# Reordering queries inside the score matmuls of an attention and channel-mix kernel

## The chip, the cores and the metric

One core of a Trainium2 chip runs the whole program. The metric is device time in microseconds (us) of one execution; a smaller number is better. The profiled execution is one run of the same program under the hardware profiler.

## What is computed

The reference is a block-causal attention followed by an RWKV channel mix, in these shapes: 8 batches, 8 heads, 576 tokens, 64 values a head; 512 channels, 1024 hidden channels.

```python
scores = (q @ k.T) / sqrt(64)                 # q, k, v: [8, 8, 576, 64]
scores = where(block_i >= block_j, scores, -1e9)   # blocks of 64 tokens
attn   = exp(scores - max) ; attn = attn / (attn.sum(-1) + 1e-9)
x      = (attn @ v).transpose(0, 2, 1, 3).reshape(8, 576, 512)
x_prev = x shifted by one token within its batch (zeros first)
xk = mu_k * x + (1 - mu_k) * x_prev
xr = mu_r * x + (1 - mu_r) * x_prev
k  = relu(xk @ w_k)                           # w_k: [512, 1024]
out = sigmoid(xr @ w_r) * ((k * k) @ w_v)     # float32 [8, 576, 512]
```

## The kernel before

**Stages.** For every batch, q and k are loaded, cast to bf16 and turned so that the 64 head values lie on the partitions. The first two batches (`TURNED = 2`) are turned by TensorE and evacuated (L462, tiles `q...` in the order list); the other six by a DMA transpose out of `NB` tiles. The result `t_qkt` holds, for every pair of heads, the queries and the keys. v is cast to fp16 into `VO`.

`add_score` makes the scores of one pair of heads in three PSUM tiles of 2 x 512 columns (`s{b}{pr}{0..2}`, L644 for the first 512 queries, L652 for the last 64), one head on the upper 64 rows of TensorE and one on the lower. The keys are the stationary operand, the queries the moving one. `J = 4` and `M = 128`: the 512 queries of a batch are cut by position p (0 to 127) and phase j (0 to 3), token = 4p + j. A piece of keys `kc` needs positions from 32 kc on, so the pieces have 512, 384, 256 and 128 columns. ScalarE takes exponentials of each tile into `t_e` in fp16 (L671), and GpSimd zeroes a masked corner (L680).

`add_values` then forms, per batch and half of the heads, the sums of the exponentials (`den`, names `d`/`e`; stationary `FOURTH` and `ONES`, four 32-column tiles of the array side by side) and three value products (`v{b}{Q}{i}`, stationary `VO`), all at L717. The sums put phase j on output partition group j, so VectorE takes reciprocals of 128 columns (L769), spreads the four phases into `t_rd` by `stream_shuffle` (L778), and `norm` (L824, L826, L813) multiplies the values by them into `t_xt`, which is float32 and in token order.

The channel mix works on chunks of 512 tokens: `d` is x minus its shift (L898, VectorE or GpSimd), `xk` and `xr` are formed on VectorE (L911), GpSimd fixes the batch borders (L926), TensorE multiplies by `WK` (L949, names `k`) and `WR` (L984, `r`), ScalarE applies relu (L960) and tanh (L995), the square (L969 or L967) goes to any of three engines, TensorE multiplies by `WV` (L1015, `p`), and VectorE joins the halves (L1027).

**Order before the change of the queries' layout.** In `t_qkt` the two turned batches hold queries in token order, and the other six hold them by phase: all positions of phase 0, then phase 1, and so on. Before, the scores and exponentials of every batch stand by phase. The turned batches therefore step through their queries four elements apart, and the others read them in a row:

```python
ask[:, 0:CUT].rearrange(
    "d (p j) -> d j p" if b < TURNED else
    "d (j p) -> d j p", j=J)[:, :, a:z],
```

The sums read each phase in a row, `probs(...)[:, j]`, and `norm` reads PSUM and `t_rd` by position and phase, 128 float32 apart, to write tokens in a row.

**What sets the order of the work.** `TENSOR` is a hand-written list of TensorE's tasks. `WHERE` says which engine does each task that could run on several (`flex`). `Plan` replays this list with a price for each task, ring buffers and semaphore latencies, and from that fixes the order of the instructions on each engine. The prices are written in the kernel (for example 0.215, 0.235 and 0.255 for the three score tiles, 0.75 for a sum of later batches). `FILL` matmuls keep TensorE occupied at the start until the first `k` task.

Of the kernel before, what the change touches and what calls it, by code (L numbers as in the profile page):

```python
# [24 lines left out]
q000 q010 q001 q011 s000 q030 q020 s0t0 s001 s010 q031 s012 s011 q021 s030 d00  # L25
s020 v000 s002 q100 q110 s022 d01 s021 q101 e00 s031 s0t1 q121 q111 v010 v001
q130 s032 q131 q120 v002 s1t0 k00 k03 e01 s100 s102 k01 v012 v011 s130 k02
s110 k04 s101 k15 s112 k06 k13 k07 s120 s111 k10 k14 k17 r01 k16 r00 k11 k05
s132 s121 k12 d10 v100 r11 s1t1 r10 s131 s122 v102 v101 p01 p10 d11 s200 v111
v110 v112 s201 s202 p00 p11 s210 s212 k20 k26 k21 s2t0 s220 r22 s211 r20 r21  # L30
r23 s230 k22 s232 k24 k23 k25 s222 k27 s221 d20 s231 p23 s2t1 v200 v201 v202
d21 s300 s302 p21 v210 v211 p20 v212 s310 s312 p22 s320 s3t0 k30 k34 k31 s330
s301 k32 k33 k35 s311 s331 r30 r33 s3t1 k37 k36 s321 s332 d30 r32 s322 r31 p31
d31 p33 p32 v300 v302 v301 v311 v312 s400 s402 v310 p30 s4t0 s420 s401 s410
k40 k43 k42 s412 s411 k41 r43 k45 k47 r42 s4t1 s422 k44 s421 k46 r40 d40 v402
v400 s430 s432 p42 s431 v401 r41 s500 d41 s501 p43 p40 v410 v411 v412 s530
s531 p41 s520 s532 r53 r52 s522 s521 k50 k56 s510 s5t1 k53 k52 k54 k57 s5t0
s512 k55 r51 k51 r50 s502 s511 d51 p50 d50 p53 s6t0 v502 v500 v510 v501 v511
s610 s611 p51 v512 s612 s6t1 p52 s600 s601 k60 k67 k64 k61 s620 s602 r60 k66
r63 k63 r61 d60 s630 s632 k65 r62 k62 s631 s621 v600 v601 v602 s622 p60 p63  # L40
s700 d61 v612 v610 v611 s701 s702 p62 s710 s711 p61 s730 s731 r70 k70 r72 s712
k72 k75 s7t0 s720 k76 r73 s7t1 s722 d70 v700 v701 s732 s721 r71 k77 k74 k73
k71 v702 d71 v710 v711 p71 p72 p73 p70 v712 k80 k84 k87 k83 k85 r81 k81 k86
k82 r83 r80 r82 p83 p82 p81 p80 r91 k90 k92 k91 k96 k94 r92 k93 k97 k95 r93
r90 p92 p90 p91 p93b p93a
# [4 lines left out]
    "ACT": "ev000 ev001 ev010 ev011 ev020 ev101 ev111 qk0000 qk0011 qk1101 "  # L50
            "qk1111 qk211 qk220 qk231 qk311 qk320 qk331 qk400 qk500 qk521 qk531 "
            "qk601 qk611 qk720 qk730 qk731 sq05 sq15 sq16 sq20 sq21 sq35 sq36 "
            "sq40 sq43 sq46 sq52 sq55 sq67 sq71 sq72 sq74 sq75 sq76 sq81 sq87 "
            "sq92 sq94 sq95 v00 v02 v03 v10 v11 v12 v30 v32 v51 v53 v60 v72 v73 "
            "wk0 wk1 wk4 wv0 wv4 wv5",
    "DVE": "d00 d01 d02 d03 d13 d20 d23 d32 d43 d50 d52 d71 d72 d81 d82 d83 "
            "d90 d91 d93 ev021 ev030 ev031 ev100 ev110 ev120 ev121 ev130 ev131 "
            "qk0010 qk0110 qk201 qk221 qk301 qk310 qk330 qk421 qk511 qk520 "
            "qk530 qk610 qk620 qk621 qk630 qk700 qk701 sq00 sq01 sq02 sq03 sq04 "
            "sq06 sq12 sq13 sq24 sq26 sq37 sq41 sq42 sq44 sq47 sq51 sq53 sq54 "  # L60
            "sq57 sq61 sq63 sq65 sq70 sq82 sq83 sq90 sq91 v01 v04 v13 v23 v31 "
            "v33 v42 v43 v44 v50 v52 v54 v61 v62 v63 wk2 wk3 wk5 wk6 wr3 wv2 "
            "wv3 wv6",
    "POOL": "d10 d11 d12 d21 d22 d30 d31 d33 d40 d41 d42 d51 d53 d60 d61 d62 "
            "d63 d70 d73 d80 d92 qk0001 qk0100 qk0101 qk0111 qk1000 qk1001 "
            "qk1010 qk1011 qk1100 qk1110 qk200 qk210 qk230 qk300 qk321 qk401 "
            "qk410 qk411 qk420 qk430 qk431 qk501 qk510 qk600 qk631 qk710 qk711 "
            "qk721 sq07 sq10 sq11 sq14 sq17 sq22 sq23 sq25 sq27 sq30 sq31 sq32 "
            "sq33 sq34 sq45 sq50 sq56 sq60 sq62 sq64 sq66 sq73 sq77 sq80 sq84 "
            "sq85 sq86 sq93 sq96 sq97 v14 v20 v21 v22 v24 v34 v40 v41 v64 v70 "  # L70
            "v71 v74 wk7 wr0 wr1 wr2 wv1 wv7",
# [7 lines left out]
class Plan:  # L79
# [15 lines left out]
    def add(self, eng, dur, fn, deps=(), takes=(), uses=(), name=None,  # L95
            mode=None, xfer=0.0, steps=0):
        t = {"eng": eng, "dur": dur, "fn": fn, "n": len(self.tasks),
             "deps": [d for d in deps if d is not None], "takes": list(takes),
             "uses": list(uses) + list(takes), "name": name, "mode": mode,
             "xfer": xfer, "key": None, "start": None, "end": None,  # L100
             "steps": 2 * steps}
        for u in t["uses"]:
            u["users"].append(t)
        for u in t["takes"]:
            u["taker"] = t
        self.tasks.append(t)
        return t
# [64 lines left out]
    def order(self, names):  # L172
# [16 lines left out]
        self.step, self.block, self.there = 0, self.FIRST, 0.0  # L189
        while any(todo.values()):  # L190
            moved, later = False, []
            for e, q in todo.items():
# [3 lines left out]
                for n, t in enumerate(q[:1] if e == "PE" else q):  # L196
# [13 lines left out]
                    if e == "PE" and t["name"][0] == "k":  # L210
                        fills.clear()
                    end = t["start"] + t["dur"]
# [64 lines left out]
def kernel(  # L277
# [95 lines left out]
    def flex(key, alts, fn, deps, takes=(), uses=()):  # L373


        eng = ENGINE.get(key, next(iter(alts)))
        t = plan.add(eng, alts[eng], lambda: fn(eng), deps, takes, uses)
        t["key"], t["alts"] = key, alts
        return t
# [42 lines left out]
    def add_turned(b):  # L422
# [6 lines left out]
        for g in range(2):  # L429
            for n in range(2):  # L430
                nl = plan.buf("nl")
                done = []
                for x in range(2):
# [8 lines left out]
                    def fn(eng, g=g, n=n, key=key, x=x):  # L442
# [9 lines left out]
                        uses=[ld] + ([nl] if x else [])))  # L452
                for y in range(2):
# [17 lines left out]
                    def ev(eng, g=g, n=n, y=y, first=first):  # L471
                        if first:
# [10 lines left out]
                             uses=[m] + ([] if first else [buf]))  # L483
# [3 lines left out]
    def add_qk(b, pr):  # L487
# [19 lines left out]
        def tail():  # L507
# [4 lines left out]
        last = on("POOL", 0.6, tail, [tl_load[b], cast["qk", b, pr, 0]],  # L512
                  uses=[nb, tiles["tlbuf", b]])
# [94 lines left out]
    def add_score(b, pr, i):  # L608
# [23 lines left out]
        def fn():  # L632
# [4 lines left out]
            for p, col, kc, a, z in mms:  # L637
                for h in range(2):
# [4 lines left out]
                    if a < M:  # L643
                        nc.tensor.matmul(  # L644
                            PS[:, h, col:col + J * w].rearrange(
                                "p (j n) -> p j n", j=J), keys,
                            ask[:, 0:CUT].rearrange(
                                "d (p j) -> d j p" if b < TURNED else
                                "d (j p) -> d j p", j=J)[:, :, a:z],
                            start=True, stop=True)  # L650
# [26 lines left out]
        def zero():  # L677
            for col, kc, a, z in pieces(b)[i]:
                if a == kc * 32 and a < M:
                    nc.gpsimd.memset(  # L680
                        tiles["e", b, pr][D:P, :, i, col:col + J * (
                            z - a)].rearrange(
                            "p h (j n) -> p h j n", j=J)[:, :, :, 0:D // J],
                        0.0)
# [4 lines left out]
    def probs(b, head, kc, a, z):  # L689
# [9 lines left out]
        if a == M:  # L699
            return E[:, 0:D]  # L700
        return E[:, 0:J * (z0 - a0)].rearrange("p (j n) -> p j n", j=J)[
            :, :, a - a0:z - a0]

    def add_values(b, Q):
# [15 lines left out]
        def sums(PS, a, z):  # L720
            kcs = [kc for kc in range(J) if kc * 32 < z]
            for j in range(J):
                for kc in kcs:
                    lo = max(a, kc * 32)
                    for g in range(G):
                        tiled(PS[:, lo - a:z - a],
                              FOURTH[:, (J - j) % J:(J - j) % J + R],
                              probs(b, 4 * Q + g, kc, lo, z)[:, j], g,
# [6 lines left out]
        def part(PS, xs, a, z):  # L735
            V = VOs[b % 2]
            wide = J * (z - a) if a < M else D
            for n, x in enumerate(xs):
                cols = slice(n * wide, n * wide + wide)
                kcs = [kc for kc in range(J) if kc * 32 < z] + [J] * (a == M)  # L740
                for kc in kcs:
                    lo = max(a, kc * 32)
                    for g in range(G):
                        ps = PS[:, cols]
                        if a < M:
                            ps = ps.rearrange("q (j n) -> q j n", j=J)[
                                :, :, lo - a:z - a]
# [4 lines left out]
        def group(name, a, z, deps, steps, dur, r_dur, s_dur):  # L752
# [23 lines left out]
            def spread():  # L776
                for j in range(J):
                    nc.vector.stream_shuffle(  # L778
                        tiles["rd", key][:, j * M + a:j * M + z],
# [3 lines left out]
        def value(i, xs, a, z, deps, steps, dur, rd, spr, key):  # L783
# [12 lines left out]
            for c, (at, wide) in enumerate(CHUNKS):  # L796
                lo = max(at, first)
                hi = min(at + wide, first + (D if a == M else J * (z - a)))
                if lo < hi:
                    scale(t, i, xs, a, z, c, lo, hi, buf, rd, spr, key)  # L800

        def scale(t, i, xs, a, z, c, lo, hi, buf, rd, spr, key):
# [5 lines left out]
            def norm():  # L808
# [3 lines left out]
                if a == M:  # L812
# [5 lines left out]
                p0, p1 = (lo - b * S) // J, (hi - b * S) // J  # L818
                num = num[:, 0:n * J * (z - a)].rearrange(
                    "q (s j p) -> q s p j", s=n, j=J)[:, :, p0 - a:p1 - a]  # L820
                r = r[:, 0:CUT].rearrange("q (j p) -> q p j", j=J)[:, p0:p1]
                x = x.rearrange("q s (p j) -> q s p j", j=J)
                if n == 1:
                    nc.vector.tensor_tensor(x[:, 0], num[:, 0], r, ALU.mult)  # L824
                else:
                    nc.vector.tensor_tensor(  # L826
                        x, num, r.unsqueeze(1).to_broadcast(
                            [P, n, p1 - p0, J]), ALU.mult)
            dur = 0.2 if a == M else 0.00118 * (hi - lo) * len(xs) + 0.02
# [7 lines left out]
        if b == 0:  # L837
            rd = group(f"d0{Q}", 0, H2, after(0), 32, 0.3, 0.5, 0.5)
            value(0, (0, 1), 0, H2, after(0), 16, 0.34, *rd)
            rd = group(f"e0{Q}", H2, M, after(0, 1, 2), 84, 0.62, 0.9, 0.5)  # L840
            value(1, (0, 1), H2, M, after(1, 2), 32, 0.78, *rd)
        else:
            rd = group(f"d{b}{Q}", 0, M, after(0, 1, 2), 84, 0.75, 1.3, 0.82)
            value(0, (0,), 0, M, after(0, 1, 2), 16, 0.56, *rd)
            value(1, (1,), 0, M, after(0, 1, 2), 16, 0.56, *rd)
        value(2, (0, 1), M, WD, after(0, 1, 2) + [ready["l", b, Q]], 40, 0.32,
# [17 lines left out]
    def add_edge(c):  # L864
# [10 lines left out]
        t = on("DVE", 0.1, edge, list(xt_parts[c - 1]),  # L875
# [6 lines left out]
    def add_mix(c, cc):  # L882
# [20 lines left out]
        for n in range(2):  # L903
# [4 lines left out]
            def mul(n=n, name=name, first=first):  # L908
# [7 lines left out]
                "DVE", 0.06 + 0.61 * f, mul, [sub] + mu_ready,  # L916
                takes=[buf] if first else [],
                uses=[d, xtbuf[h]] + ([] if first else [buf])))
# [3 lines left out]
            for b in range(B):  # L922
                at = b * S - CHUNKS[c][0]
                if 0 < at < w:
                    def fix(n=n, at=at, name=name):
# [5 lines left out]
                        "POOL", 0.25, fix, list(mixed[c, n]),  # L931
                        uses=[buf, xtbuf[h]]))
# [193 lines left out]
```

## Time and profile before

| | |
|---|---|
| median of 3 runs | 291.16 us (290.99 to 293.34) |
| profiled execution | 293.19 us, its span 291.4 us |
| mean granted TensorE clock | 0.953 |
| TensorE busy | 260.1 us (89%), 4136 matmuls |
| VectorE / ScalarE / GpSimd busy | 214.2 / 190.7 / 133.8 us |
| exponentials, L671 | 96 of 1026 ns, 95.4 us |
| scores, L644 | 272 matmuls, 35.6 us busy |
| sums and values, L717 | values of L717 on `t_e`, `VO`: 1056 matmuls, 28.5 us busy |
| norms, L824 | 56 of 596 ns, 30.9 us |

Rows of the profile name a line, an engine, an operation, the tiles (out<-in), a form and a count, then busy time and the mean length of one. Matmuls overlap in the array, so the length of one is longer than its share of time; the distance between starts is what it costs in a row of work. Lines are those of the kernel before.

### The profile page before, as it was taken

The numbers are of one execution on the slowest core, as the hardware profiler recorded it, in microseconds if no ns is written. First come the engines' busy times: TensorE is split into PE (matmuls) and PEld (weight loads), VectorE is DVE, ScalarE is ACT, GpSimd is POOL, SyncE is SP. The second block draws the span as 40 slices with busy tenths as digits, with TensorE's granted clock in tenths as the row PEclk, the third lists the DMA queues.
The fourth block names the chain that finished last, engine by engine and source line by source line (L and its number), as shares of the span: only waits on it lengthen the run. The fifth ranks groups of instructions, "written<-read, shape, count | busy, mean of one in ns | idle before, by whom it ended". The sixth has DMA issues, their size and how long they took to land. (4 is left out here: it accounts for less than half of the span.)

```text
span 291.4 us, 10011 instructions
## 1 busy us (share of the span) xinstructions
PE 260.1 (89%) x4136; PEld 133.7 (46%) x4136; DVE 214.2 (74%) x484; ACT 190.7 (65%) x297; POOL 133.8 (46%) x274
## 2 busy tenths in 40 slices
PE   0997889988999899959999999979979989969995
PEld 0765646553345345513454346435443544423443
DVE  2379997699439947896499768995898399993303
ACT  2997589954995599166974894649748960540560
POOL 3362548845485487363342550658643150540030
PEclk9996599999999999986999999979999999997999
DMA  7999996799999999999948999978941100301203
GB/s 225 313 302 237 308 257 199 162 227 198 250 260 175 207 289 238 207 140 284 250 86 170 249 229 203 240 227 170 135 119 37 40 2 2 144 0 53 94 0 145
DMA packets 118301, 51.51 MB, mean 177 GB/s; under 512 B 102768, under 2 KB 109168, under 8 KB 118256
## 3 DMA queue, kind: packets, MB, share of 16 engines
q1 hardware_dynamic: 118256, 50.88, 75.2%
q8 instruction: 32, 0.52, 0.7%
q14 instruction: 13, 0.11, 0.1%
HBM read 33.56 MB, written 9.44 MB: 148 GB/s over the span
## 5 line engine op out<-in xcount | busy, mean ns | idle before, releaser
L671 ACT ACTIVATE t_e<-t_s 128x1024 f16<-128x1024 f32 x96 | 95.4, 1026 | 33.2 <-PE t_s L644 25.1
L949 PE MATMUL t_mm<-t_xk,WK 128*128 128x512 f16 (+1 forms) x320 | 74.9, 378 | 8.6 <-POOL t_xk L926 4.0
L1015 PE MATMUL t_mm<-WV,t_k 128*128 128x512 f16 (+1 forms) x296 | 68.0, 381 | 6.5 <-DVE t_k L969 3.3
L960 ACT ACTIVATE t_kr<-t_mm 128x512 f32<-128x512 f32 (+1 forms) x80 | 43.4, 559 | 30.0 <-PE t_mm L949 26.8
L949 PEld LDWEIGHTS <-WK 128*128 128x128 f16 x320 | 30.5, 102 | 43.9 <-issue 11.1
L1015 PEld LDWEIGHTS <-t_k 128*128 128x128 f16 x296 | 27.9, 99 | 39.5 <-issue 6.0
L969 POOL TENSOR_TENSOR t_k<-t_kr 128x512 f16<-128x512 f32 (+1 forms) x30 | 32.7, 1100 | 27.6 <-ACT t_kr L960 27.3
L680 POOL MEMSET t_e<- 64x128 f16 x128 | 24.5, 213 | 45.2 <-ACT t_e L671 42.0
L898 POOL TENSOR_TENSOR t_d<-t_xt 128x512 f32<-128x512 f32 (+1 forms) x21 | 24.6, 1176 | 40.7 <-DVE t_xt L824 27.5
L969 DVE TENSOR_TENSOR t_k<-t_kr 128x512 f16<-128x512 f32 (+1 forms) x27 | 19.8, 740 | 25.0 <-ACT t_kr L960 25.0
L984 PE MATMUL t_mm<-WR,t_xr 128*128 128x512 f16 x144 | 36.5, 380 | 0.5 <-DVE t_xr L911 0.3
L1027 DVE SCALAR_TENSOR_TENSOR t_o<-t_t,t_mm 128x512 f32<-128x512 f32 (+1 forms) x37 | 24.4, 665 | 16.8 <-PE t_mm L1015 13.9
L644 PE MATMUL t_s<-t_qkt 64*128 64x256 bf16 (+3 forms) x272 | 35.6, 328 | 0.5 <-ACT t_e L671 0.5
L911 DVE SCALAR_TENSOR_TENSOR t_xk<-t_d,MUK,t_xt 128x512 f16<-128x512 f32 (+1 forms) x40 | 33.4, 861 | 0.4 <-POOL t_d L898 0.3
L911 DVE SCALAR_TENSOR_TENSOR t_xr<-t_d,MUR,t_xt 128x512 f16<-128x512 f32 (+1 forms) x40 | 32.7, 843 | 0.0
L824 DVE TENSOR_TENSOR t_xt<-t_mm,t_rd 128x448 f32<-128x448 f32 (+6 forms) x56 | 30.9, 596 | 1.8 <-PE t_mm L717 1.2
L717 PE MATMUL t_mm<-t_e,VO 128*32 128x64 f16 (+4 forms) x1056 | 28.5, 252 | 2.7 <-DVE t_o L1027 1.9
L995 ACT ACTIVATE t_t<-t_mm 128x512 f32<-128x512 f32 x36 | 21.1, 605 | 13.6 <-PE t_mm L984 13.5
L769 DVE RECIPROCAL t_c<-t_mm 128x128 f32<-128x128 f32 (+1 forms) x18 | 15.5, 861 | 14.2 <-PE t_mm L717 14.2
L717 PEld LDWEIGHTS <-VO 128*32 128x32 f16 x1184 | 19.5, 99 | 12.3 <-issue 5.9
L652 PE MATMUL t_s<-t_qkt 64*128 64x64 bf16 x320 | 23.9, 197 | 0.3 <-ACT EL L659 0.3
L984 PEld LDWEIGHTS <-t_xr 128*128 128x128 f16 x144 | 13.1, 98 | 16.5 <-issue 1.5
(60 smaller groups left out, 274.6 us busy)
## 6 DMA issues: line engine op xcount, KB each, us to landing
out_dram<-t_o SPq DMA_DIRECT2D x35, 256.0 KB, 3.3
t_vl<-in_v_dram SPq DMA_DIRECT2D x32, 256.0 KB, 4.9
t_ld<-in_k_dram SPq DMA_DIRECT2D x48, 128.0 KB, 4.0
t_ld<-in_q_dram SPq DMA_DIRECT2D x24, 256.0 KB, 4.3
t_ld<-in_q_dram SPq DMA_DIRECT2D x8, 288.0 KB, 5.1
t_ld<-in_k_dram SPq DMA_DIRECT2D x8, 288.0 KB, 6.1
t_ld<-in_moe_w_k_dram SPq DMA_DIRECT2D x8, 256.0 KB, 5.3
t_ld<-in_moe_w_v_dram SPq DMA_DIRECT2D x8, 256.0 KB, 3.2
```

What stands on the lines that cost most here:

```text
L644: nc.tensor.matmul(PS[:, h, col:col + J * w].rearrange("p (j n) -> p j n", j=J), keys, ask[:, 0:CUT].rearrange("d (p j) -> d j p" if b < T ...
L671: nc.scalar.activation(tiles["e", b, pr][:, :, i, :], tiles["ps", b, pr, i], AF.Exp, scale=ISQ)
L680: nc.gpsimd.memset(tiles["e", b, pr][D:P, :, i, col:col + J * (z - a)].rearrange("p h (j n) -> p h j n", j=J)[:, :, :, 0:D // J], 0.0)
L717: nc.tensor.matmul(ps[g * R:g * R + R], lhs, e, start=start, stop=stop, tile_position=(0, g * R))
L824: nc.vector.tensor_tensor(x[:, 0], num[:, 0], r, ALU.mult)
L898: (nc.vector if eng == "DVE" else nc.gpsimd).tensor_tensor(tiles["d", c, cc][:, 0:w], x[:, cc, o + 1:o + w + 1], x[:, cc, o:o + w], ALU.su ...
L911: nc.vector.scalar_tensor_tensor(tiles[name, h][:, cc, o:o + w], tiles["d", c, cc][:, 0:w], (MUK1, MUR1)[n][:, cc:cc + 1], xt_tile(c)[:, c ...
L949: nc.tensor.matmul(ps[:, 0:w], WK[:, cc, jc * P:(jc + 1) * P], tiles["xk", h][:, cc, o:o + w], start=(cc == 0), stop=(cc == CCn - 1))
L960: nc.scalar.activation(tiles["kr", c, jc][:, 0:w], tiles["pk", c, jc][:, 0:w], AF.Relu)
L969: (nc.vector if eng == "DVE" else nc.gpsimd).tensor_tensor(K2, KR, KR, ALU.mult)
L984: nc.tensor.matmul(ps, tiles["xr", h][:, cc, o + jt * P:o + (jt + 1) * P], WR[:, cc], start=(cc == 0), stop=(cc == CCn - 1))
L1015: nc.tensor.matmul(ps[:, 0:w], tiles["k2", h][:, jc, off:off + P], WV[:, jc, cols], start=(jc == 0), stop=(jc == JCn - 1))
```

## The change

Scores, exponentials and values now stand in token order. The turned batches read their queries in a row; the other six read them by position and phase, four phases 128 bf16 apart for every position. The sums take every fourth exponential. The spread writes `t_rd` four float32 apart, and the norm reads and writes in a row. The masked corner is one run of 64.

The plan gets a `lock` argument, given to most tasks that may stand on VectorE or GpSimd: in the replay such a task does not start while a locked task of the other engine runs. Some prices in the plan change; those of the scores do not. `TENSOR` and `WHERE` are new lists with the same names of tasks; no instruction is issued by the lock itself.

```diff
@@ TENSOR, WHERE: new order of the same tasks, new engines for part of them
...
-            mode=None, xfer=0.0, steps=0):
+            mode=None, xfer=0.0, steps=0, lock=()):
...
+                    if e in t["lock"]:
+                        t["start"] = max(now, *[
+                            port[x] for x in port if x != e], 0.0)
+                        port[e] = t["start"] + t["dur"]
...
-                        nc.tensor.matmul(
-                            PS[:, h, col:col + J * w].rearrange(
-                                "p (j n) -> p j n", j=J), keys,
-                            ask[:, 0:CUT].rearrange(
-                                "d (p j) -> d j p" if b < TURNED else
-                                "d (j p) -> d j p", j=J)[:, :, a:z],
-                            start=True, stop=True)
+                        moving = ask[:, J * a:J * z]
+                        dst = PS[:, h, col:col + J * w]
+                        if b >= TURNED:
+                            moving = ask[:, 0:CUT].rearrange(
+                                "d (j p) -> d p j", j=J)[:, a:z]
+                            dst = dst.rearrange("k (p j) -> k p j", j=J)
+                        nc.tensor.matmul(dst, keys, moving, start=True,
+                                         stop=True)
...
-                        tiles["e", b, pr][D:P, :, i, col:col + J * (
-                            z - a)].rearrange(
-                            "p h (j n) -> p h j n", j=J)[:, :, :, 0:D // J],
-                        0.0)
+                        tiles["e", b, pr][D:P, :, i, col:col + D], 0.0)
...
-        return E[:, 0:J * (z0 - a0)].rearrange("p (j n) -> p j n", j=J)[
-            :, :, a - a0:z - a0]
+        return E[:, J * (a - a0):J * (z - a0)]
...
-                              probs(b, 4 * Q + g, kc, lo, z)[:, j], g,
+                              probs(b, 4 * Q + g, kc, lo, z)[:, j::J], g,
...
-                            ps = ps.rearrange("q (j n) -> q j n", j=J)[
-                                :, :, lo - a:z - a]
+                            ps = ps[:, J * (lo - a):J * (z - a)]
...
-                        tiles["rd", key][:, j * M + a:j * M + z],
+                        tiles["rd", key][:, J * a + j:J * z:J],
...
-                num = num[:, 0:n * J * (z - a)].rearrange(
-                    "q (s j p) -> q s p j", s=n, j=J)[:, :, p0 - a:p1 - a]
-                r = r[:, 0:CUT].rearrange("q (j p) -> q p j", j=J)[:, p0:p1]
-                x = x.rearrange("q s (p j) -> q s p j", j=J)
...
+                    "p (s t) -> p s t", s=n)[:, :, lo - first:hi - first]
+                r = r[:, lo - b * S:hi - b * S]
+                nc.vector.tensor_tensor(
+                    x, num, r.unsqueeze(1).to_broadcast([P, n, hi - lo]),
+                    ALU.mult)
...
```

## Prediction

> **What bounds the kernel now.** I read the busy shares and the clock by slices first, then the waits of TensorE, then the busy time by stretches between clock changes, and last the groups split by form.
>
> ```profile
> PE 260.1 (89%) x4136; PEld 133.7 (46%) x4136; DVE 214.2 (74%) x484; ACT 190.7 (65%) x297; POOL 133.8 (46%) x274
> PEclk9996599999999999986999999979999999997999
> ```
>
> TensorE is busy for 89% of the span, no other engine for more than 74%. The clock digits fall to 5 or 6 in four places; the stretches below put them at half clock. The chain that ended last is almost all TensorE too. Its long waits:
>
> ```profile
> PE t_mm L462 <- POOL t_nl L390: 6.8, 1, 6.8
> PE t_mm L949 <- POOL t_xk L926: 4.0, 3, 2.2
> PE t_mm L949 <- DVE t_xt L824: 3.5, 2, 2.8
> PE t_mm L1015 <- DVE t_k L969: 3.3, 1, 3.3
> ```
>
> The first is the start. The others are the mix of x waiting for VectorE and GpSimd. By stretches (columns: length; busy time of PE, PEld, DVE, ACT, POOL with counts; clock; DMA share, GB/s):
>
> ```profile
> 57.50:129.70 72.20, 65.87 (x1151) 32.40 (x1140) 56.62 (x124) 49.78 (x74) 43.00 (x86) 1.00 1.09 222
> 129.70:136.50 6.80, 5.68 (x22) 2.04 (x24) 5.25 (x12) 2.80 (x5) 2.76 (x7) 0.50 0.90 244
> 136.50:191.10 54.60, 51.39 (x921) 25.48 (x918) 43.74 (x101) 40.35 (x61) 22.11 (x52) 1.00 0.94 210
> 191.10:194.50 3.40, 3.40 (x9) 1.23 (x9) 3.40 (x8) 0.60 (x1) 1.16 (x3) 0.50 1.00 276
> 194.50:232.00 37.50, 35.28 (x642) 17.71 (x640) 27.08 (x60) 30.51 (x46) 19.56 (x43) 1.00 0.55 101
> ```
>
> From 57.5 to 232 us, where the six DMA-turned batches run, TensorE works 161.6 of 174.5 us: 12.9 us are idle, and half clock wastes about half of 5.68 + 3.40, 4.5 us. So at most 17.4 us can be won there by better cover; work added to TensorE beyond that lengthens the run.
>
> **What stepping costs in this trace.** The before kernel has both kinds of score reads. The first two rows are a turned batch (queries 8 bytes apart) at 45 to 57 us, the other two the DMA-turned batches at 60 to 232 us (in a row); then two norms and a norm of contiguous operands:
>
> ```profile
> L644 PE MATMUL t_s<-t_qkt 64*128 64x512 bf16 x2 | 0.6, 608 | 0.0
> L644 PE MATMUL t_s<-t_qkt 64*128 64x128 bf16 x4 | 0.6, 272 | 0.0
> ...
> L644 PE MATMUL t_s<-t_qkt 64*128 64x512 bf16 x48 | 9.3, 385 | 0.5 <-ACT t_e L671 0.5
> L644 PE MATMUL t_s<-t_qkt 64*128 64x128 bf16 x48 | 5.4, 220 | 0.0
> ...
> L824 DVE TENSOR_TENSOR t_xt<-t_mm,t_rd 128x448 f32<-128x448 f32 x8 | 7.4, 930 | 0.3
> L824 DVE TENSOR_TENSOR t_xt<-t_mm,t_rd 128x64 f32<-128x64 f32 x8 | 2.0, 254 | 0.0
> L813 DVE TENSOR_TENSOR t_xt<-t_mm,t_rd 128x128 f32<-128x128 f32 x16 | 4.5, 282 | 0.1
> L390 DVE COPY t_qkt<-t_mm 128x576 bf16<-128x576 bf16 x9 | 6.6, 742 | 3.7 <-PE t_mm L462 3.7
> ```
>
> (608 - 272)/384 = 0.87 ns a column stepped, (385 - 220)/384 = 0.43 in a row: an 8-byte step halves the read at full clock. The norm costs (930 - 254)/384 = 1.76 ns an element with both inputs 512 bytes apart. The copy reads PSUM just as scattered (64 bf16 apart) and takes 742 ns for 576, so the norm's stepped `t_rd` in SBUF is the likelier cause.
>
> [...]
>
> **The change, part by part.**
>
> *Turned batches' scores.* Per pair of heads 1280 columns (the two heads side by side), 5120 a batch. Reading in a row saves 0.43 x 5120 = 2.2 us a batch. Part of batch 0 runs at half clock (23.9 to 37.5 us), where a contiguous read is no faster than a stepped one. I take -3 of -4.4.
>
> *The other six batches' scores.* 6 x 5120 = 30,720 columns, now one query per 256 bytes with four lines in rotation. The trace of before doesn't show this on TensorE. Lower bound of the cost: nothing. At the step that is shown (0.87): +0.44 x 30,720 = +13.5. At a line for each query (1.7): +1.27 x 30,720 = +39. I take +39: the norm, too, walks four lines in rotation, the same shape as the new queries, and gets nothing from coming back to them.
>
> *Sums.* 14 groups of later batches have 4 x (128 + 96 + 64 + 32) columns; now fp16 with an 8-byte step. [...] 1152 columns x 0.43 = 0.5 us a group on top of the 0.77 us now (52.21 to 52.98), 7.0 for 14, and batch 0 adds 0.9. Four tiles stream side by side, which the stepped scores don't show: bounds 0 and +8. I take +7.
>
> *Values.* Both are contiguous moving reads; PSUM writes become contiguous; 0, bound -1. *Masked corners*: the same 128 elements in 199 ns; 0, bounds -2 and +1 on GpSimd, which is 46% busy.
>
> *Norms.* At 128 elements the contiguous form takes 282 against 366 ns: -0.66 ns each, x 16,384 = -10.8 us of VectorE; about -0.3 us for the 448 form. *Spreads* [...] 72 shuffles, 8192 elements x 0..0.7 ns = 0 to +5.8; I take +3. VectorE nets -8. None of this is on TensorE; it shortens the waits before `k`, a norm at a time.
>
> *New engines.* ScalarE gains 7 casts of q and k, 9 squares and 3 evacuations and loses a few, by their rows about +9 (191 to 200, 69%). GpSimd loses 4 subtractions, 6 casts and 3 squares and gains weight and v casts, about -12. VectorE is near even, 4 subtractions more but 6 v casts fewer. No engine comes near TensorE. [...] L911 is (947 - 740) x 32 + (936 - 740) x 32 = 13 us over its quiet length. That is cover, not TensorE time. SP issues the same loads, transposes and stores in another order; the DMA share is near 1 until 200 us, but hardly a wait of TensorE ends in a DMA, and a slower TensorE gives DMAs more time.
>
> *New order.* The fixed list was timed with 0.215 to 0.255 for score tiles; at 1.7 ns a column the 512-column tile takes 0.87. Everything queued behind it on TensorE (`k`, `r`, `p`, sums) waits, while VectorE, GpSimd and ScalarE catch up. Two score tiles in PSUM against a 1.03 us exponential: TensorE still makes a tile faster than ScalarE takes it, so ScalarE does not become the bound. With 46 us more on TensorE and 8 less on VectorE, I expect about 60% of the 17.4 us of idle and half clock to go: -11. The chain sum to norm to mix after a batch stays, so not all goes.
>
> **Sum**, on the profiled execution's own 293.19 us (span 291.4 and 1.8 around it): -3 + 39 + 7 - 11 = +32, 325 us. It ran 2.0 above the median of the runs: 323 us as such a median.
>
> **Rivals.** A change within 1% is about what a measurement here can't tell from none.
>
> *A. A stepped read costs two, whatever the step.* The stepped score rows are at exactly twice[...], and the norm's 1.76 comes from PSUM. Against it: the copy out of PSUM. -3 + 13.5 + 7, and less cover, -7: +10, 301 us.
>
> *B. TensorE rides over the large step (faster).* [...] the sums' four streams hide their step. Place: L644 of batches 2 to 7. Then -3 from scores, -3 from shorter norms before `k` and `p`, -1 from a half-clock stretch that isn't entered: 284 us. It decides if a column costs under about 0.5 ns. For it: only that the rows don't show this step. Against it: even 8 bytes cost twice.
>
> *C. Reads are free as in B, but the new order loses the gain.* Each long wait in the list starts a half-clock stretch of 3.4 us or more, which wastes 1.7; two more such waits of 2 us cost 7 and end at 291.
>
> **Chances.** Main case 0.48 (308 to 335), A 0.28 (295 to 308), B 0.16, C 0.08. Faster is B, 0.16; same is most of C, 0.06; slower the rest, 0.78. The main case's own range comes from recovered cover of 5 to 17 and sums of 0 to 8. For 8 in 10 the range reaches down through A to 289 and up to 335.
>
> **What would show it.** L644 with 512 columns in batches 2 to 7: about 1050 ns in the main case (385 + 512 x 1.3), 610 in A, 385 in B; the turned batches' 512 at 385. Sums of 84 matmuls in about 1.25 us. Norms of 448 near 630, shuffles 290 to 380. TensorE's waits between 57 us and the last score well under 12 us. If L644 doesn't grow, the forecast is wrong at its first step; if it grows and the span doesn't, cover was larger than 17 us.

## The result, and the profile after

The changed kernel takes 314.72 us (median of 4 runs, 313.89 to 315.38) against 292.25 us for the kernel before on the same chip: a ratio of 1.077, 95% interval 1.070 to 1.083. It is slower, by 22 us. The profiled execution took 314.58 us with a span of 312.8, so 21.4 us more span than before. An execution more than 1.5% above the fastest of its kernel counts as slow, and the ratios below compare the others.

The page of the changed kernel, first the busy shares and the clock by slices:

```profile
PE 294.1 (94%) x4120; PEld 139.5 (45%) x4120; DVE 220.5 (71%) x477; ACT 202.1 (65%) x313; POOL 114.1 (36%) x265
PEclk9998699999999999999999999999999999999999
```

TensorE is busy for 34.0 us more (294.1 against 260.1), and idle for 12.6 us less (18.7 against 31.3). One slow place is left in the clock, where there were four. Work was added to TensorE, and part of it was covered: time that had been lost to waits and to half clock was won back. By stretches (columns as before: length, busy PE, PEld, DVE, ACT, POOL, clock, DMA):

```profile
29.30:36.10 6.80, 5.39 (x183) 3.80 (x186) 6.52 (x17) 4.66 (x7) 4.49 (x10) 0.50 1.09 284
...
57.50:265.00 207.50, 205.31 (x2748) 86.82 (x2749) 142.76 (x297) 140.54 (x209) 79.68 (x184) 1.00 0.73 162
```

From 57.5 to 265 us, six us past the last score, TensorE waits 2.2 us in 207.5, where it waited 12.9 in 174.5 up to the last score before. The score matmuls of batches 2 to 7 (60 to 265 us), then the longest of the sums, the spread and the norm of the changed kernel; below the last dots, the sum and the spread of the kernel before:

```profile
L657 PE MATMUL t_s<-t_qkt 64*128 64x512 bf16 x46 | 23.5, 1019 | 0.0
L657 PE MATMUL t_s<-t_qkt 64*128 64x128 bf16 x46 | 8.7, 375 | 0.0
...
L721 PE MATMUL t_mm<-t_e,FOURTH 128*32 128x128 f16 x224 | 16.6, 281 | 0.0
L781 DVE STREAM_SHUFFLE t_rd<-t_c 128x128 f32<-128x128 f32 x56 | 36.9, 946 | 0.0
L825 DVE TENSOR_TENSOR t_xt<-t_mm,t_rd 128x448 f32<-128x448 f32 x8 | 4.9, 613 | 0.1
...
L717 PE MATMUL t_mm<-t_e,FOURTH 128*32 128x128 f16 x224 | 10.0, 220 | 0.2 <-issue 0.2
L778 DVE STREAM_SHUFFLE t_rd<-t_c 128x128 f32<-128x128 f32 x56 | 12.8, 292 | 0.0
```

The scores cost (1019 - 375)/384 = 1.68 ns a column, four times the 0.43 of before. The norm fell from 930 to 613 ns as meant, and the shuffle, whose price nobody meant to change, rose from 292 to 946. In order of time (start, length, what), two shuffles of one spread before and two after:

```profile
54.81 0.30 DVE L778 STREAM_SHUFFLE t_rd<-t_c 128x128 f32<-128x128 f32 x1
55.02 0.30 DVE L778 STREAM_SHUFFLE t_rd<-t_c 128x128 f32<-128x128 f32 x1
```

```profile
116.58 0.01 DVE L781 LOAD_MASK_SELECT t_rd<-t_c  x1
116.58 1.01 DVE L781 STREAM_SHUFFLE t_rd<-t_c 128x128 f32<-128x128 f32 x1
117.22 0.02 DVE L781 LOAD_MASK_SELECT t_rd<-t_c  x1
117.22 1.01 DVE L781 STREAM_SHUFFLE t_rd<-t_c 128x128 f32<-128x128 f32 x1
```

Shuffles follow each other 0.21 us apart before and 0.64 after; the lengths overlap, so the distance of starts is the price.

### The profile page after: what moved, and what is told of

Same layout as the page of the kernel before. It is cut to its first block, busy times and chain, and to the rows that moved or that the text cites. A ratio compares the mean times of both kernels' runs of the same rounds, so it can differ in the third digit from the quotient of the medians.

```text
span 312.8 us, 9964 instructions
## 1 busy us (share of the span) xinstructions
PE 294.1 (94%) x4120; PEld 139.5 (45%) x4120; DVE 220.5 (71%) x477; ACT 202.1 (65%) x313; POOL 114.1 (36%) x265
## 4 chain that ended last, share of the span: by engine, by line
PE 80%; DVE 12%; ACT 4%; issue 2%; DMA 1%; SPq 0%; POOL 0%; DVEq 0%; ACTq 0%
PE t_mm L948 19%; PE t_s L657 17%; PE t_mm L1014 17%; PE t_mm L721 13%; PE t_mm L983 10%; DVE t_rd L781 5%; ACT t_e L679 3%; PE t_s L660 2%; DVE t_xt L825 2%; DMA t_ld<-in_q_dram 1%; PE t_mm L469 1%; DVE t_c L772 1%; DVE t_d L897 1%; DVE t_xk L910 1%; DVE t_rd L775 1%
## 5 line engine op out<-in xcount | busy, mean ns | idle before, releaser
L657 PE MATMUL t_s<-t_qkt 64*128 64x128 bf16 (+3 forms) x272 | 71.2, 588 | 1.5 <-ACT t_e L679 1.4
L948 PE MATMUL t_mm<-t_xk,WK 128*128 128x512 f16 (+1 forms) x320 | 69.1, 359 | 1.9 <-DVE t_xt L825 1.2
L781 DVE STREAM_SHUFFLE t_rd<-t_c 128x128 f32<-128x128 f32 (+1 forms) x72 | 42.8, 868 | 0.0
L968 POOL TENSOR_TENSOR t_k<-t_kr 128x512 f16<-128x512 f32 (+1 forms) x27 | 26.1, 974 | 31.5 <-ACT t_kr L959 31.4
L983 PE MATMUL t_mm<-WR,t_xr 128*128 128x512 f16 x144 | 35.9, 380 | 0.0
L968 DVE TENSOR_TENSOR t_k<-t_kr 128x512 f16<-128x512 f32 (+1 forms) x24 | 17.6, 743 | 23.1 <-ACT t_kr L959 23.1
L910 DVE SCALAR_TENSOR_TENSOR t_xk<-t_d,MUK,t_xt 128x512 f16<-128x512 f32 (+1 forms) x40 | 28.8, 747 | 1.7 <-POOL t_d L897 1.6
L910 DVE SCALAR_TENSOR_TENSOR t_xr<-t_d,MUR,t_xt 128x512 f16<-128x512 f32 (+1 forms) x40 | 29.8, 770 | 0.0
L660 PE MATMUL t_s<-t_qkt 64*128 64x64 bf16 x320 | 27.7, 204 | 1.1 <-ACT t_e L679 1.1
L825 DVE TENSOR_TENSOR t_xt<-t_mm,t_rd 128x448 f32<-128x448 f32 (+7 forms) x60 | 23.6, 436 | 4.1 <-PE t_mm L721 3.0
L657 PEld LDWEIGHTS <-t_qkt 64*128 64x128 bf16 x272 | 13.8, 101 | 27.5 <-issue 25.1
```

The costliest lines, as they stand in the source:

```text
L657: nc.tensor.matmul(dst, keys, moving, start=True, stop=True)
L660: nc.tensor.matmul(PS[:, h, col:col + D], keys, ask[:, CUT:S], start=True, stop=True)
L781: nc.vector.stream_shuffle(tiles["rd", key][:, J * a + j:J * z:J], tiles["c", key][:, 0:z - a], [j] * 32)
L825: nc.vector.tensor_tensor(x, num, r.unsqueeze(1).to_broadcast([P, n, hi - lo]), ALU.mult)
L910: nc.vector.scalar_tensor_tensor(tiles[name, h][:, cc, o:o + w], tiles["d", c, cc][:, 0:w], (MUK1, MUR1)[n][:, cc:cc + 1], xt_tile(c)[:, c ...
L948: nc.tensor.matmul(ps[:, 0:w], WK[:, cc, jc * P:(jc + 1) * P], tiles["xk", h][:, cc, o:o + w], start=(cc == 0), stop=(cc == CCn - 1))
```

## The experiments

### One step taken out at a time

**Scores in a row.** The permutation of the six batches' queries is dropped.

```diff
                         moving = ask[:, J * a:J * z]
                         dst = PS[:, h, col:col + J * w]
-                        if b >= TURNED:
-                            moving = ask[:, 0:CUT].rearrange(
-                                "d (j p) -> d p j", j=J)[:, a:z]
-                            dst = dst.rearrange("k (p j) -> k p j", j=J)
```

> The changed kernel, but all batches read their queries in a row in the scores; the reordering of the six DMA-turned batches' queries is left out, nothing else. Theory ([...] TensorE is the bound): the 512-column form of L657 falls from about 945 to 385 ns on average, TensorE's score time falls by 36 us, some idle and half clock comes back (5 to 12 us), the median falls from 314.7 to 284-291. Rival 1 (the new chain reciprocal, stepped spread, norm on VectorE sets the end): no more than 5 us fall, 309-314. Rival 2 (the new order of work costs the time): L657 gets shorter and the time stays above 303.

Measured: 285.7 us, 0.976 of the kernel before (0.971 to 0.981). Its busy shares:

```profile
PE 256.1 (90%) x4120; PEld 138.8 (49%) x4120; DVE 220.5 (78%) x477; ACT 198.7 (70%) x313; POOL 116.6 (41%) x265
```

TensorE's busy time falls by 38.0 us (294.1 to 256.1) and the time by 29; idle rises from 18.7 to 27.9. The theory's number holds. VectorE is as busy as in the changed kernel, to the tenth, with all its slow shuffles, and the run is 29 us shorter, so VectorE's chain did not set the end of the changed kernel.

**Sums in a row.**

```diff
-                              probs(b, 4 * Q + g, kc, lo, z)[:, j::J], g,
+                              probs(b, 4 * Q + g, kc, lo, z)[
+                                  :, j * (z - lo):(j + 1) * (z - lo)], g,
```

> The changed kernel, but the sums read each quarter of the exponentials in a row instead of every fourth one; so the sums are of the wrong tokens, the amount of work is the same. Theory: a sum of 84 matmuls falls from 1.33 to 0.77 us where nothing interrupts it, 9 us in all, and the time falls by 6 to 9 us, to 306-309. Rival 1 (VectorE's chain sets the end): a fall of 3 us or less, 311-315. Rival 2 (order): as rival 1.

Measured: 308.0 us, ratio 1.052 (1.047 to 1.058); TensorE is busy 285.9 us, 8.2 less. So the step of the sums costs 8.2 us of TensorE and 6.7 us of time.

**Spread in a row**, norm stepped in SBUF alone.

```diff
-                        tiles["rd", key][:, J * a + j:J * z:J],
+                        tiles["rd", key][:, j * M + a:j * M + z],
...
-                r = r[:, lo - b * S:hi - b * S]
+                p0, p1 = (lo - b * S) // J, (hi - b * S) // J
+                r = r[:, 0:CUT].rearrange("q (j p) -> q p j", j=J)[:, p0:p1]
+                num = num.rearrange("q s (p j) -> q s p j", j=J)
...
```

> The changed kernel, but the spread writes the four phases in a row again, and the norm reads them by position and phase, 512 bytes apart, while values in PSUM and the result stay in a row. Theory (TensorE is the bound, VectorE's stepped spread is mostly covered): shuffles of 128 fall from 946 to 292 ns, 27 us less of VectorE; if the norm's step in SBUF is what made it slow before, its 448 form returns to 930 ns (about 10 us more in all), if it was PSUM it stays at 613. The time falls by 1 to 6 us, 309-314. Rival 1 (the chain on VectorE sets the end): 290-302.

Measured: 311.05 us, ratio 1.062 (1.057 to 1.068). Its rows:

```profile
L781 DVE STREAM_SHUFFLE t_rd<-t_c 128x128 f32<-128x128 f32 x56 | 12.8, 296 | 0.0
L829 DVE TENSOR_TENSOR t_xt<-t_mm,t_rd 128x448 f32<-128x448 f32 x8 | 7.5, 932 | 1.0 <-PE t_mm L721 0.7
```

The norm is back at 932 ns although it reads PSUM in a row: the access to SBUF alone brings the price back, and the step in PSUM that the kernel before had too (930 ns) adds nothing to it. VectorE works 16.1 us less (204.4), and the time falls by 3.7: the slow shuffles are mostly covered, although the chain that ended last in the changed kernel runs through them for 5.1% of the span, 16 us.

**All three in a row**, with the spread as blocks in token positions.

> The changed kernel with every step left out: scores, sums and spread all in a row (the tokens' reordering is left out in the first two, and the spread's phases stand in the wrong places); norms in a row as in the change. It bounds what the idea could give if stepping were free. Theory: from 285.7 (scores in a row) another -9 for the sums and up to -8 for waits on VectorE: 266-274, at or a little below the old layout under the same plan (272).

Measured: 268.3 us (268.1 and 268.5; two more executions took 272.2 and 275.0). So even with free steps the new layout would come out, under this plan, at most some 4 us below the old layout under it (272 us, shown further down), and two executions are few for a difference of that size.

### What a step costs

Each of the six later batches gets its own step in the scores, and batches 2 to 5 their own way of spreading.

```diff
+                        elif b == 3:
+                            nc.tensor.matmul(to(2), keys, by(2), **kw)
+                        elif b == 4:
+                            nc.tensor.matmul(to(4), keys, by(4), **kw)
...
+                    if b == 2:
+                        nc.vector.stream_shuffle(R[:, j * M:j * M + M], c, [j] * 32)
...
+                    elif b == 4:
+                        nc.vector.tensor_copy(R[:, j:J * M:J], c)
+                    elif b == 5:
+                        nc.vector.tensor_copy(R[:, j * M:j * M + M], c)
```

> The changed kernel with another step in each of the DMA-turned batches, each on a line of its own, so tokens are exchanged within a piece and, in batches 4 and 5, the spread is a plain copy; its time as a whole says nothing. Scores: batch 2 in a row, 3 with 2 elements (4 bytes), 4 with 4 (8 bytes), 5 with 8 (16 bytes), 6 with 16 (32 bytes), 7 as the change has it (256 bytes, four lines in rotation). Line theory, ns a column between the 512- and 128-column forms: 0.42, 0.42, 0.83, 1.65, 1.65, 1.65. Rival A (any step costs two): 0.42 in a row and 0.83 for all others. Spread: batch 2 in a row 292 ns; 3 with 8 bytes; 6 and 7 with 16 bytes 720-1020; batch 4 a copy with 16 bytes, batch 5 a copy in a row. If the stepped write is slow for any instruction, the copy of batch 4 takes 700-1000; if it is the shuffle's own, below 350.

The score groups of this kernel; L661 steps by 4 bytes, L663 by 8, L665 by 16, L667 by 32, L669 by 256 with four lines in rotation:

```profile
L661 PE MATMUL t_s<-t_qkt 64*128 64x512 bf16 x8 | 1.6, 391 | 0.2 <-ACT t_e L693 0.2
L661 PE MATMUL t_s<-t_qkt 64*128 64x128 bf16 x8 | 0.9, 216 | 0.0
L663 PE MATMUL t_s<-t_qkt 64*128 64x512 bf16 x8 | 2.4, 607 | 0.0
L663 PE MATMUL t_s<-t_qkt 64*128 64x128 bf16 x8 | 1.1, 272 | 0.0
L665 PE MATMUL t_s<-t_qkt 64*128 64x512 bf16 x8 | 4.2, 1056 | 0.0
L665 PE MATMUL t_s<-t_qkt 64*128 64x128 bf16 x8 | 1.5, 383 | 0.0
...
L667 PE MATMUL t_s<-t_qkt 64*128 64x512 bf16 x8 | 4.3, 1073 | 0.0
L667 PE MATMUL t_s<-t_qkt 64*128 64x128 bf16 x8 | 1.6, 386 | 0.0
L669 PE MATMUL t_s<-t_qkt 64*128 64x512 bf16 x8 | 4.1, 1019 | 0.0
```

From the 128- to the 512-column form, per column: 0.46, 0.87, 1.75, 1.79 ns, and 1.68 for the rotation (374 at 128 columns). A 4-byte step is nearly free (0.43 in a row), the price doubles at 8 and again at 16, and then stays. Rival A, two for any step, falls at both ends. From 8 bytes on the prices are as if each 16 bytes touched cost about 1.75 ns. That describes these figures, and no run shows what lies behind it; the "line" of the recorded texts is such a stretch of 16 bytes, the author's estimate from 2 x 0.87 = 1.74 ns of TensorE at 8 bytes beside the norm's 1.76.

The shuffle and the copy, L797 in a row, L800 at 8 bytes, L806 at 16 (batches 1, 6 and 7), copies at 16 bytes (L802) and in a row (L804):

```profile
L797 DVE STREAM_SHUFFLE t_rd<-t_c 128x128 f32<-128x128 f32 x8 | 1.8, 296 | 0.0
L800 DVE STREAM_SHUFFLE t_rd<-t_c 128x128 f32<-128x128 f32 x8 | 2.9, 514 | 0.0
L806 DVE STREAM_SHUFFLE t_rd<-t_c 128x128 f32<-128x128 f32 x24 | 15.8, 941 | 0.0
...
L802 DVE COPY t_rd<-t_c 128x128 f32<-128x128 f32 x8 | 1.2, 259 | 0.0
L804 DVE COPY t_rd<-t_c 128x128 f32<-128x128 f32 x8 | 1.1, 204 | 0.0
```

A copy that writes every fourth word takes 259 ns against 204; the shuffle 941 against 296. So the slow stepped write belongs to the shuffle here, and not to every instruction of VectorE.

### The layout apart from the plan

**Old layout under the new plan.** Order list, engines, prices and lock are those of the change, all layout hunks are undone.

```diff
-                        moving = ask[:, J * a:J * z]
...
+                            ask[:, 0:CUT].rearrange(
+                                "d (p j) -> d j p" if b < TURNED else
+                                "d (j p) -> d j p", j=J)[:, :, a:z],
...
```

> The plan of the changed kernel (order list, engines, lock, prices) with the layout of the kernel before (scores, exponentials and values by phase, norm stepped). Theory (the stepped reads on TensorE are the whole loss, the plan is neutral or a little better): 283-294 us. Rival 2 (the new order costs the time): 300 or more. Against the kernel before, the clear difference would be the waits of TensorE, 28 us idle and 27 us at half clock before.

Measured: 272.13 us, ratio 0.929 (0.925 to 0.934). The expectation of "neutral or a little better" was too low: with the old layout the plan is worth 7%.

```profile
PE 248.9 (92%) x4120; PEld 129.6 (48%) x4120; DVE 203.8 (76%) x477; ACT 198.0 (74%) x313; POOL 115.9 (43%) x265
PEclk9999999999999999999999999999999999999999
```

No slice shows half clock (the second profile of this kernel, further down, has one stretch of it, near 93 us), and TensorE's idle is 20.3 us (269.2 span less 248.9) where it was 31.3. Between this kernel and the changed one only the layout differs: TensorE is busy 45.2 us longer, the span is 43.6 us longer.

**New layout under the old plan**, its hunks put into the kernel before.

> The layout of the changed kernel (stepped queries, stepped sums, stepped spread) with the order list, engines, prices and lock-free plan of the kernel before. Theory (the layout adds 36 + 9 us to TensorE, and its waits can cover part of it): the cost of the layout under the old order is 30-45 us, so 322-337. If the loss were one of the new order: near 293-300.

Measured: 328.2 us, ratio 1.119 (1.113 to 1.125). The layout alone costs 35 us here (328.2 against 293.1) and 43 under the new plan; here TensorE's idle falls from 31.3 to 25.8 us and half clock gets rarer, so part of the added work is covered; there hardly anything was left to give.

**Which part of the plan.** All three in the old layout: the new lists with the old prices and no lock; the old lists with the new prices and lock; and the whole again. `port`, in the code and in the texts below, is the replay's own note of when the locked task of each engine ends.

> The kernel before with the new order list and the new engines, but its own plan: no lock, old prices; the layout of before. Theory (the lists carry the gain; the plan only sorts the other engines' queues by due time): 271-277. Rival (the plan's knowledge of the port carries it): 284 or more.

> The kernel before with its own order list and engines, but the plan of the change (lock and new prices); the layout of before. Theory (the lists carry the gain): 288-294, no difference from before that matters. Rival (the plan carries it): 280 or less.

> The old layout under the whole plan of the change again, on the same chip as the two others, timed more closely, since it is the best kernel so far: 271-273, ratio to the kernel before 0.925-0.935.

Measured ratios: 0.981 (0.973 to 0.988), 1.008 (1.005 to 1.012) and 0.934 (0.930 to 0.939). The second kernel spread from 290.5 to 299.6 us, and over all its twenty executions the ratio of medians is 1.016, so it gains nothing either way. The first run (285.2 us) came out where the rival put it, the second where the theory did, and neither account fits both: the lists alone give about 2%, the plan on the old lists gives nothing, and only together they give 7%. A last kernel keeps the new lists and prices and leaves the lock out of the replay:

```diff
-                    if e in t["lock"]:
-                        t["start"] = max(now, *[
-                            port[x] for x in port if x != e], 0.0)
-                        port[e] = t["start"] + t["dur"]
```

> The old layout, the new order list and engines and the new prices, but the plan's replay has no lock for the port; it differs from the 271.5 us kernel by that alone. The lists alone gave 285.2, the whole plan 271.5. If the lock carries what the plan adds: 281-286. If the new prices carry it: 270-274. Between 274 and 281: both.

Measured: 279.9 us, ratio 0.958 (0.953 to 0.963). So with the new lists the prices are worth some 2%, and the lock, which issues no instruction, another 2%. TensorE's idle is 30.5 us with the lists alone, 24.3 with the prices too and 19.5 with the whole plan. Its longest waits after that of the start, first with the new lists alone, then with the whole plan:

```profile
PE t_s L643 <- DMA t_qkt<-NB: 5.0, 1, 5.0
PE t_mm L716 <- DVE t_qkt L389: 2.7, 1, 2.7
PE t_mm L716 <- POOL t_e L679: 1.9, 2, 1.7
```

```profile
PE t_s L651 <- DMA t_qkt<-NB: 2.7, 2, 2.5
PE t_mm L957 <- DVE t_xt L832: 1.9, 3, 1.2
PE t_s L659 <- ACT t_e L678: 1.5, 2, 1.2
```

A reading that fits, but that no run isolates: the lists assume an arrival for everything, and with the plan that they were written for, the other engines' queues come out in an order that meets them. Less slowing of VectorE beside GpSimd can be a small part. In the trace of before, the 64 instructions of L911 on 512 columns, `xk` and `xr`, take 643 to 746 ns with no GpSimd instruction beside them (26), 645 to 751 beside memsets alone (6), and 737 to 1546, on average 1148, beside any other (32). `xk` of 512 columns averages 816 ns with the lists alone, 813 with prices too and 802 with the lock, `xr` 865, 826 and 789, so 32 of each save about 3 us of VectorE in all. The rest is most likely which task stands ahead of which; that was not isolated.

### A version between the two

Token order in the two turned batches alone, where queries then read in a row, in the old layout and the new plan:

```diff
+                        moving = ask[:, J * a:J * z]
+                        dst = PS[:, h, col:col + J * w]
+                        if b >= TURNED:
+                            moving = ask[:, 0:CUT].rearrange(
+                                "d (j p) -> d j p", j=J)[:, :, a:z]
+                            dst = dst.rearrange("k (j p) -> k j p", j=J)
...
```

> The old layout with the plan of the change (272 us), but the two turned batches alone have scores, exponentials and values in token order: their scores read in a row (-2.2 us a batch), their sums step by 8 bytes (+1.1 in batch 1, about +1 in batch 0), the spread stays in a row and the norm steps in SBUF only. Theory: -2 us of TensorE, most of it before 60 us where other waits stand: 269-273. If a wait on ScalarE or on loads bounds this stretch: no change, 272.

Measured: 272.4 us, ratio 0.931 (0.926 to 0.937): no difference from the old layout's 0.929 and 0.934 that the intervals show. TensorE is busy 247.8 us against 248.9, and its idle is 22.4 against 20.3. The old layout under the new plan, at 272 us, and this version are the best kernels of the study that keep the tokens' order, 7% ahead of the kernel before and 13.5% ahead of the changed one.

## Why the prediction was right, and where its terms were off

The forecast was 323 us with a range of 289 to 335, which took in rival A as well; the time is 314.7, in the main case's own 308 to 335. The forecast change was +32, the measured one +22.

- *Six batches' scores, +39.* Right in place and size: 1.68 ns a column where 1.7 was taken, 38.0 us of TensorE's time in the run with scores in a row. The 1.7 was an estimate that joined two engines' prices, the norm's 1.76 ns and twice the 8-byte step's 0.87 on TensorE. The spread-in-a-row run bears out its weakest link, that the norm's price came from SBUF and not from PSUM (932 ns with PSUM read in a row, 930 before), and the ladder shows TensorE's price at 16 bytes directly, 1.75. That the two engines' figures agree was luck in part: nothing in the trace of before tied them, and the shuffle, which also steps by 16 bytes, pays 5 ns (0.64 us for 128).
- *Turned batches' scores, -3.* Right: in the version between the two, all the scores but the last 64 queries' take 32.5 us of TensorE against 35.9.
- *Sums, +7.* Measured 8.2. What failed is leaving the 32-column sets out of the 1152 columns: their matmuls, too, grew from 179 to 211 ns. The miss is small, and part of it is rounding: the parts named, 7.0 and 0.9, come to 7.9, and 7 was taken. The 84 matmuls of a sum took 1.33 us from the first start to the first of the values (234.89 to 236.22 us) where they took 0.77. That four streams run side by side hid nothing: 0.56 us more, where 0.5 was taken.
- *Together on TensorE*, scores and sums less the turned batches' gain: +43 in the sum, 45.2 between the two layouts under one plan.
- *Norms, -10.8.* Right: L824 and L826 took 35.0 us before, L825 takes 23.6.
- *Spreads, +3, bounds 0 to 5.8.* Wrong by far, outside its bounds: 42.8 us against 15.4 (12.8 and 2.6), +27. The bound took a write to cost at most what a stepped read does; the trace of before had no stepped shuffle, and the ladder shows a price of its own, 941 ns at 16 bytes against 296 in a row. With it the forecast that "VectorE nets -8" fails: VectorE is busy 220.5 us where the old layout under the same plan takes 203.8. It did little harm, 3.7 us of time, because TensorE was by then the bound even more than before.
- *Cover and order, -11 of at most 17.4.* Wrong in size. Between 57.5 us and the last score the idle fell from 12.9 to 2.2 us and the half clock went: about 15 where 11 was taken. Outside that stretch the prediction expected nothing, and there some 7 us more came back. The first stretch of half clock shrank from 13.6 to 6.8 us, and the wait of 3.3 us near 260 us is gone, with the half clock behind it; the prediction read that wait as one for the mix of x, but it was one for a square (L969). The reason given, that slower scores let the other engines catch up, is tested by the new layout under the old plan. There the loss in that stretch came down from 17.4 to about 6.4 us (4.9 idle in 209.5, and 4.0 of work at a clock of 0.61), just the 11 forecast. So the reason was right in size, and what the prediction put at nothing is the new plan, which it set aside with "That is cover, not TensorE time". With the old layout the plan saves 22.2 us of span, with the new layout 13.5 (326.3 to 312.8): its gain and that of the added work do not add, since both draw on the same idle and half clock. In sum, by spans: the plan with the old layout -22.2, from 291.4 to 269.2 (forecast for cover: -11), and the layout on top of it +43.6 (forecast +43); that is the 10 us between the 325 of the sum and the profiled 314.6.
- *Rival A* is excluded by the ladder, *B* by the 1019 ns, and *C* by the same 1019 ns and by the plan, which wins. The link of half clock to long waits that C used is not general: of TensorE's four longest waits before, those of 2.2, 2.8 and 3.3 us stand at the beginning of a stretch of half clock (3.4, 6.8 and 3.4 us long), and the longest, 6.8 us at the start, does not.

## What to carry to other kernels

Read the price of an access pattern from the same kernel where two patterns stand side by side, and follow it up to the step that is meant; here twice the 8-byte price of the scores, 1.74 ns, gave that of 16, 32 and 256 bytes (1.75, 1.79 and 1.68), but the norm's 1.76 ns did not carry over to the shuffle's write (5 ns), so an instruction whose stepped form the trace does not show needs a run of its own. Moving a reorder from VectorE, which had slack, to the moving operand of TensorE, which had little, lost; here it did not even lighten VectorE, since the norms' 11 us less were outweighed by the shuffles' 27 more. When a layout and a plan change at once, run each with the other's old half: here a gain of 7% was hidden under a loss of 15 to 16%.

## What was not expected of the hardware

- A moving bf16 read steps by 4 bytes for almost nothing (0.46 ns a column against 0.43), and costs 0.87, 1.75 and 1.79 at 8, 16 and 32 bytes.
- In the stretches at half clock (granted 0.50) a score matmul of 512 columns takes as long with its queries in a row as at an 8-byte step, 618 ns after (4 matmuls) against 610 before (2); the stepped one is no slower there than at full clock, 608. At 128 columns, before, the two take 292 (2) and 289 (4).
- `stream_shuffle` of 128 columns writes in 296 ns in a row, 514 at an 8-byte and 941 at a 16-byte step; a copy of the same shape takes 204 in a row and 259 at 16 bytes.
